# Projecting K and Q of the first token pair one tile at a time, and retuning the planner, in a fused transformer layer

## The chip, the cores and the metric

The kernel runs on one core of one Trainium2 chip. The metric is the device time of one execution in microseconds (us). A run is one execution; a profiled execution also leaves a trace, and its span is some 2 us shorter than its time. Engine names: PE is TensorE, DVE is VectorE, ACT is ScalarE, SP is the queue that issues the DMAs. The profile also records the clock that PE was granted, as a share of the full one; in these runs it is 1.00 or 0.50.

## The reference

One pre-norm transformer layer on 2048 tokens of 1024 columns with 32 heads of 32 columns, and a feed-forward part (FFN) of 3584 columns. Everything is bf16.

```python
def _A_ref(x, wqkv, wo):
    qkv = (x @ wqkv).reshape(B, S, 3, H, Dh)          # H = 32, Dh = 32; cut
    scores = jnp.einsum("bhqd,bhkd->bhqk", q, k) * Dh ** -0.5
    o = jnp.einsum("bhqk,bhkd->bhqd", _softmax(scores), v)
    return o.reshape(B, S, D) @ wo                     # transposes cut
def _B_ref(x, w1, b1, w2, b2):
    return _gelu(x @ w1 + b1) @ w2 + b2
h = x + _A_ref(_layernorm(x), A_wqkv, A_wo)
return h + _B_ref(_layernorm(h), B_w1, B_b1, B_w2, B_b2)
```

## The kernel before

The kernel is a program generator. Python code lists tasks for all engines with estimated durations. A planner then simulates them and fixes the order of instructions on each engine. So a changed estimate can move thousands of instructions, and the diff alone doesn't show which.

Queries are handled in chunks of 256 tokens. A *round* is 8 score matmuls (keys of two token tiles, into PSUM) and two exponentials of 128x1024 on ACT. There are 1024 exponentials. `PT` names the exponentials, and *PV* is their product with V, again on PE. A tile is 128 tokens. The beginning of the program (the *lead*) takes tokens in pairs of tiles: layer norm, transposes (`xnT`), K and Q of the first head group (`KT`, `QT`), V, then a round. `proj_k` and the like take a start column and a width: 256 columns are both tiles.

```python
    jobs = [Job(0, 0, 6, True), Job(0, 1, 5, True)]     # PSUM banks 6 and 5
    for i in range(8):
        ...                                             # cut: layer norm of tiles 2i, 2i+1
        for tt in tts:
            trs.append(tr_tile(tt, "act" if i in ACT_T else "dma"))
        proj_k(group("lead", FULL), 0, 256 * i, 256, "act")      # both tiles at once
        if i < 2:
            q = group("lead", FULL)
            proj_q(q, 0, 256 * i, 256, i, "dve")
        v = group("lead", FULL)
        ...
        proj_v(v, 2 * i, 0, "act")
        jobs[0].round()
```

Later, work of the FFN fills PE between the rounds. Its second matmul (FFN2) reads the weights `w2r` from a ring of 7 slots, one DMA of 512 KB each. One output half `j` needs FC // 4 = 7 such blocks; the two token tiles `t` share them. `PLAN` says in which order the FFN2 groups (`F2[0]` to `F2[3]`, as `(j, t)`) and blocks of the first FFN matmul (the numbers say how many) are offered to PE. `AHEAD` is a look-ahead in us of the planner's own time: a group of matmuls may be begun when its operands will be ready that soon. (The expectations below call it a share.)

```python
    NW1, NW2 = 4, 7
    F2 = [(0, 0), (0, 1), (1, 0), (1, 1)]
    PLAN = [F2[0], 3, F2[1], 4, F2[2], 5, F2[3], 2]
    ...
    def ffn2(R, c, j, t, tail=False):
        if t == 0:
            w2s[c, j] = [w2block(R.w2, B_w2[512 * q:512 * q + 512, 512 * j:512 * j + 512]) for q in range(FC // 4)]
    ...
    AHEAD = 0.15
    ...                                                 # cut, in the planner's choice for PE:
        p.left == 0 and p.ready <= now + AHEAD and all(x.done is not None for x in p.gate)
        and all(x.left == 0 for x in p.dmas)
```

The softmax here doesn't subtract the row's maximum and nothing guards it: scores larger than these inputs give would overflow.

Of the kernel before, what the change touches and what calls it, by code (L numbers as in the profile page):

```python
# [12 lines left out]
P = 128  # L13
# [299 lines left out]
def build_kernel(nc, A_x, A_wqkv, A_wo, B_w1, B_b1, B_w2, B_b2, out):  # L313
# [17 lines left out]
    gr = Graph(N_LANES)  # L331
# [68 lines left out]
    F2 = [(0, 0), (0, 1), (1, 0), (1, 1)]  # L400
# [51 lines left out]
    B_ps = [gr.buf() for _ in range(8)]  # L452
# [5 lines left out]
    hd = nc.dram_tensor("h_scratch", [NC - 1, 2, P, D], BF, kind="Internal").ap()  # L458
    B_hd = [[gr.buf() for _ in range(2)] for _ in range(NC - 1)]

    MM = 0.2150

    def c_dve_ps(n):
        return (120 + n) / 960.0 + 0.02
# [4 lines left out]
    def c_act(n, ap_bias=False):  # L469
        return 0.072 + (0.093 if ap_bias else 0.0) + n / 1200.0  # L470

    EXP = (0.9163, 0.9013)

    def pe(fns, occ, reads=(), writes=(), kind="bg", mode="full", prio=0, after=()):
        return gr.add(E.PE, fns, occ, 0.16, reads, writes, prio, kind, mode, after)
# [3 lines left out]
    def group(name, full=False):  # L479
        g = Group((1, len(groups)), gr.buf())  # L480
        g.full = full
        g.after = ()
        g.name = name
        groups.append(g)
        return g
# [6 lines left out]
    def mm(g, lhsT, rhs, start, stop, reads, cols=(0, 512)):  # L492
        c0, c1 = cols
        occ = MM * (c1 - c0) / 512.0 + 0.0015
        fns = []
        k = rhs.shape[1] if len(rhs.shape) == 3 else 1

        def dst(a, b):
            o = psum[a:b, g.bank, c0:c1]
            return o if k == 1 else o.rearrange("p (k n) -> p k n", k=k)  # L500
        for j in range(4):
            fns.append(lambda p, j=j: p.matmul(dst(32 * j, 32 * j + 32), lhsT[:, 32 * j:32 * j + 32], rhs,  # L502
                                               start=start, stop=stop, tile_position=(0, 32 * j), skip_group_check=True))
        t = grp_pe(g, fns, occ, reads, "col")
        t.alt = [lambda p: p.matmul(dst(0, P), lhsT, rhs, start=start, stop=stop, skip_group_check=True)]  # L505
        if g.full:
            t.fns, t.mode = t.alt, "full"
# [82 lines left out]
    def evacuate(eng, dst, src, n, reads, writes):  # L590
        if eng == "act":
            act(lambda a: a.activation(dst, src(), ACT.Copy), n, reads=reads, writes=writes, prio=-1)  # L592
        else:
            dve(lambda v: v.tensor_copy(dst, src()), c_dve_ps(n), reads=reads, writes=writes, prio=-2)  # L594
# [11 lines left out]
    def x_tile(tt, prio):  # L606
        ap, b = x_slot(tt)
        return dma(ap, x2[tt * P:(tt + 1) * P, :], P * D * 2, writes=b, prio=prio)

    def ln_tiles(tts, prio, on_act=(), after=()):  # L610
        return layer_norm([x_slot(tt) + (xb[:, tt % NXB, :], B_xb[tt % NXB]) for tt in tts], prio, on_act, after)

    def tr_tile(tt, evac):
        if evac != "dma":
            transposes(group("lead", True), xb[:, tt % NXB, :], B_xb[tt % NXB], xnT[:, tt, :, :], B_xnT[tt], evac)
            return
        return dma_t(xnT[:, tt, :, :], xb[:, tt % NXB, :], [B_xb[tt % NXB]], [B_xnT[tt]], prio=-6)

    def proj(grp, which, g, t0, n, col, start=True):
        blk, c = divmod(g * P, 512)  # L620
        blk += WQ if which == 0 else WK
        a, b = t0 // P, (t0 + n) // P
        for dc in range(DC):
            mm(grp, Wall[:, blk, dc, c:c + P], xnT[:, a:b, dc, :], start and dc == 0, dc == DC - 1,
               [B_W[blk][c // P]] + B_xnT[a:b], cols=(col, col + n))

    def proj_k(grp, g, t0, n, evac):
        proj(grp, 1, g, t0, n, 0)
        evacuate(evac, KT[:, g, t0:t0 + n], lambda: psum[:, grp.bank, 0:n], n, [grp.buf], B_KT[g][t0 // 256:(t0 + n) // 256])

    def proj_q(grp, g, t0, n, slot, evac):
        proj(grp, 0, g, t0, n, 0)
        k = n // 256
        evacuate(evac, QT[:, slot:slot + k, :], lambda: psum[:, grp.bank, 0:n].rearrange("p (s t) -> p s t", s=k), n,
                 [grp.buf], B_QT[slot:slot + k])

    def proj_v(grp, tt, q, evac):
        blk, c = divmod(256 * q, 512)
        blk += WV
        for k in range(2):  # L640
            for dc in range(DC):
                mm(grp, xnT[:, tt + k, dc, :], Wall[:, blk, dc, c:c + 256], dc == 0, dc == DC - 1,
                   B_W[blk][c // P:c // P + 2] + [B_xnT[tt + k]], cols=(256 * k, 256 * k + 256))
        dst = V[:, 2 * q:2 * q + 2, tt:tt + 2, :].rearrange("p g t c -> p t g c")
        evacuate(evac, dst, lambda: psum[:, grp.bank, :].rearrange("p (t g c) -> p t g c", t=2, g=2), 512,
                 [grp.buf], [B_V[2 * q][tt // 2], B_V[2 * q + 1][tt // 2]])
# [30 lines left out]
    class Job:  # L677
# [10 lines left out]
        def round(self):  # L688
# [18 lines left out]
            for q in range(2):  # L707
                u = us[q]
                t = act(lambda a, u=u, q=q: a.activation(PT[:, s, 2 * q:2 * q + 2, :], psum[:, 2 * u:2 * u + 2, :], ACT.Exp, bias=0.0, scale=SCALE),  # L709
                    1024, reads=[B_ps[2 * u], B_ps[2 * u + 1]], writes=[B_PT[s][q]], kind="exp")  # L710
                t.occ = EXP[q]
            direct = self.direct or (self.final and r == 7)
# [76 lines left out]
    def wo(R, c):  # L789
        for j in range(2):  # L790
            ws = wo_w(R, j)
            for t in range(2):
                wo_group(R, c, j, t, ws)
# [14 lines left out]
    def ln2(R, c, evac):  # L808
        for t in range(2):
            ln2_tile(R, c, t, evac)  # L810
# [72 lines left out]
    def mixed(R, c1, c2, plan):  # L883
        blk = 0
        for p in plan:
            if isinstance(p, int):
                ffn1(R, c1, range(blk, blk + p))
                blk += p
            else:
                ffn2(R, c2, *p)  # L890
# [22 lines left out]
    for i in range(8):  # L913
        tts = [2 * i, 2 * i + 1]
        if i == 0:
            ln_tiles(tts[:1], LEAD_PRIO)
            first = ln_tiles(tts[1:], LEAD_PRIO, (0,))
        else:
            ln_tiles(tts, 0, (), first)
        for tt in tts:  # L920
            trs.append(tr_tile(tt, "act" if i in ACT_T else "dma"))
            if tt + NXR < NT:
                last_x = [x_tile(tt + NXR, -4)]
        proj_k(group("lead", FULL), 0, 256 * i, 256, "act")
        if i < 2:
            q = group("lead", FULL)
            proj_q(q, 0, 256 * i, 256, i, "dve")
        v = group("lead", FULL)
        if i == 0:
            v.after = q.buf.w  # L930
        proj_v(v, 2 * i, 0, "act")
        jobs[0].round()
        if i == 1:
            jobs[1].round()
        if i >= 1:
            jobs[1].round()
# [30 lines left out]
    def projections(g):  # L967
        proj_q(group(f"pq{g}"), g, 0, 512, slot_of(g, 0), "dve")
        for tc in range(4):
            proj_k(group(f"pk{g}"), g, 512 * tc, 512, "dve")  # L970
        if g > 1:
            for tt in range(0, NT, 4):
                proj_v1(group(f"pv{g}.{tt}", True), tt, g, "dve")
# [20 lines left out]
    def attention(c):  # L994
        for g in range(G):
            attend(g, c)
            c2, g2 = divmod(G * c + g + NQ, G)
            if c2 < NC:
                load_q(g2, c2)

    PLAN = [F2[0], 3, F2[1], 4, F2[2], 5, F2[3], 2]
    wo(R1, 1)
    ffn1(R1, 0, range(FC // 2))
    for c in range(2, NC):
        if c > 2:
            wo(R1, c - 1)
        ln2(R1, c - 1, "dma")
        mixed(R1, c - 1, c - 2, PLAN)
        attention(c)
# [11 lines left out]
    k = R1.w1.k % NW1  # L1021
# [30 lines left out]
    g_next = [0]  # L1052
    qks = [t for t in gr.tasks if t.kind == "qk"]
    PV_START = 6
    AHEAD = 0.15
    HOLD = 3

    def full_array(t):
# [2 lines left out]
    def pick_pe(rd, now, state, up):  # L1061
# [20 lines left out]
        for t in rd:  # L1082
# [10 lines left out]
            else:  # L1093
                p = t.grp
                if p.bank is None and (not new_ok or not ((p is first and n >= len(pvs)) or (
                        p.left == 0 and p.ready <= now + AHEAD and all(x.done is not None for x in p.gate)
                        and all(x.left == 0 for x in p.dmas)))):
# [25 lines left out]
        return warm  # L1123

    num = {t: i for i, t in enumerate(gr.tasks)}
    gr.schedule(pick_pe, switch=0.11382196630878494)

    sems = {e: nc.alloc_semaphore(f"f_{e.name}") for e in (E.PE, E.Activation, E.DVE, E.Pool)}
    lanes = [nc.alloc_semaphore(f"f_lane{i}") for i in range(N_LANES)]
# [28 lines left out]
def bass_sequential_preLN__softmax_full_mha__dense_activation_gelu__prompt_kernel(  # L1158
    nc: bass.Bass,
    A_x: bass.AP,  # L1160
    A_wqkv: bass.AP,
    A_wo: bass.AP,
    B_x: bass.AP,
    B_w1: bass.AP,
    B_b1: bass.AP,
    B_w2: bass.AP,
    B_b2: bass.AP,
    out: bass.AP,
):
    build_kernel(nc, A_x, A_wqkv, A_wo, B_w1, B_b1, B_w2, B_b2, out)  # L1170
# [28 lines left out]
```

## Time and profile before

The median was 1099.68 us in 3 runs (1098.5 to 1100.67). The profile was read in three stages, marked by the exponentials in ACT's timeline:

| stage, kernel before | from where to where | us |
|---|---|---|
| lead | start to the start of the 33rd exponential, from which on ACT is fed | 63.26 |
| middle | to the end of the 1024th exponential (1022.50) | 959.24 |
| tail | to the end of the span (1096.5) | 74.03 |

Three lines of the page matter besides those that the prediction shows: the shares of the chain that ended last by engine, the group of FFN2's matmuls (after the last bar: idle time of PE before them, and what ended most of it), and the loads of FFN2's weights (KB each, median us from issue to landing).

### The profile page before, as it was taken

The numbers are of one execution on the slowest core, as the hardware profiler recorded it, in microseconds if no ns is written. First come the engines' busy times: TensorE is split into PE (matmuls) and PEld (weight loads), VectorE is DVE, ScalarE is ACT, GpSimd is POOL, SyncE is SP. The second block draws the span as 40 slices with busy tenths as digits, with TensorE's granted clock in tenths as the row PEclk, the third lists the DMA queues.
The fourth block names the chain that finished last, engine by engine and source line by source line (L and its number), as shares of the span: only waits on it lengthen the run. The fifth ranks groups of instructions, "written<-read, shape, count | busy, mean of one in ns | idle before, by whom it ended". The sixth has DMA issues, their size and how long they took to land.

```text
span 1096.5 us, 41949 instructions
## 1 busy us (share of the span) xinstructions
PE 1062.1 (97%) x19130; PEld 589.0 (54%) x19135; DVE 822.9 (75%) x1449; ACT 1021.6 (93%) x1135; POOL 17.8 (2%) x33
## 2 busy tenths in 40 slices
PE   7999999999999989999999999999999999999999
PEld 6545555554444655554555455455545544554485
DVE  7456666767767998788788788877887888887562
ACT  5889999999999999999999999999999999999351
POOL 1000000000000000000000000000000000000000
PEclk9999999999999999999999999999999999999999
DMA  7960100013444755577838856765778477968860
GB/s 197 195 159 3 51 3 3 3 41 92 120 122 127 210 133 162 183 242 150 271 113 254 218 169 185 210 208 153 234 162 255 136 224 205 311 186 261 248 224 20
DMA packets 269211, 176.52 MB, mean 161 GB/s; under 512 B 51434, under 2 KB 265066, under 8 KB 269034
## 3 DMA queue, kind: packets, MB, share of 16 engines
q1 hardware_dynamic: 269034, 173.84, 55.4%
q8 instruction: 150, 2.46, 0.9%
q14 instruction: 27, 0.22, 0.1%
HBM read 155.98 MB, written 11.01 MB: 152 GB/s over the span
## 4 chain that ended last, share of the span: by engine, by line
ACT 83%; PE 15%; DMA 1%; DVE 1%; issue 0%; POOL 0%; POOLq 0%; DVEq 0%
ACT PT L709 79%; PE ps L505 8%; ACT a_sq L850 4%; PE ps L502 3%; PE ps L701 1%; PE ps L721 1%; DMA hnT<-xb 1%; PE ps L907 1%; PE ps L740 1%; DVE PS L716 0%; ACT xnT L584 0%; PE ps L581 0%; DVE gT L851 0%; ACT V L592 0%; DVE a_os L878 0%
## 5 line engine op out<-in xcount | busy, mean ns | idle before, releaser
L709 ACT ACTIVATE PT<-ps 128x1024 bf16<-128x1024 f32 x1024 | 953.8, 1164 | 12.7 <-PE ps L701 12.4
L716 DVE TENSOR_TENSOR PS<-PT 128x1024 bf16<-128x1024 bf16 x495 | 327.6, 686 | 83.1 <-ACT PT L709 49.5
L701 PE MATMUL ps<-QT,KT 32*128 32x256 bf16 x4096 | 203.9, 273 | 13.5 <-ACT PT L709 11.5
L505 PE MATMUL ps<-hnT,w1r 128*128 128x256 bf16 x1632 | 209.5, 274 | 2.1 <-DVE gT L832 0.6
L502 PE MATMUL ps<-w2r,gT 128*32 128x512 bf16 x2880 | 192.8, 383 | 1.9 <-issue 0.8
L721 PE MATMUL ps<-PT,V 128*32 128x256 bf16 x4096 | 180.9, 275 | 5.9 <-ACT PT L709 5.0
L505 PEld LDWEIGHTS ps<-hnT,w1r 128*128 128x128 bf16 x1632 | 146.2, 98 | 57.0 <-issue 36.2
L701 PEld LDWEIGHTS ps<-QT,KT 32*128 32x128 bf16 x4096 | 61.3, 92 | 163.5 <-ACT PT L709 141.7
L740 PE MATMUL ps<-PS,ones 128*32 128x256 bf16 x1980 | 139.4, 276 | 2.3 <-DVE PS L716 1.5
L502 PE MATMUL ps<-xnT,Wall 128*32 128x512 bf16 x1888 | 126.0, 381 | 1.3 <-DVE stg L594 1.2
L721 PEld LDWEIGHTS ps<-PT,V 128*32 128x32 bf16 x4096 | 94.4, 96 | 54.5 <-ACT PT L709 24.0
L502 PEld LDWEIGHTS ps<-w2r,gT 128*32 128x32 bf16 x2880 | 67.4, 96 | 71.2 <-issue 26.7
L832 DVE TENSOR_TENSOR gT<-ps,b1f 128x512 bf16<-128x512 f32 x98 | 67.4, 687 | 25.7 <-PE ps L505 24.5
L740 PEld LDWEIGHTS ps<-PS,ones 128*32 128x32 bf16 x1980 | 51.7, 96 | 40.6 <-DVE PS L716 23.4
L505 PE MATMUL ps<-Wall,xnT 128*128 128x128 bf16 (+1 forms) x896 | 69.3, 227 | 0.7 <-ACT xnT L584 0.7
L851 DVE SCALAR_TENSOR_TENSOR gT<-a_sq,gT 128x1024 bf16<-128x1024 bf16 x49 | 59.9, 1222 | 12.3 <-ACT a_sq L850 11.8
L502 PEld LDWEIGHTS ps<-xnT,Wall 128*32 128x32 bf16 x1888 | 43.5, 96 | 46.5 <-issue 15.0
L505 PEld LDWEIGHTS ps<-Wall,xnT 128*128 128x128 bf16 x896 | 55.2, 98 | 16.3 <-issue 10.7
L502 PE MATMUL ps<-w1r,OT 128*32 128x512 bf16 x896 | 62.2, 381 | 0.5 <-DVE OS L752 0.2
L848 DVE SCALAR_TENSOR_TENSOR a_sq<-a_sq,gT 128x1024 bf16<-128x1024 bf16 x49 | 59.8, 1221 | 0.7
L850 ACT ACTIVATE a_sq<-a_sq 128x1024 bf16<-128x1024 bf16 x49 | 58.9, 1203 | 0.0
L749 DVE STREAM_TRANSPOSE DT<-ps 128x256 f32<-128x256 f32 x64 | 28.5, 445 | 20.1 <-PE ps L740 20.1
(76 smaller groups left out, 570.7 us busy)
## 6 DMA issues: line engine op xcount, KB each, us to landing
w2r<-in_B_w_dram SPq DMA_DIRECT2D x105, 512.0 KB, 6.0
w1r<-in_B_w_dram SPq DMA_DIRECT2D x102, 512.0 KB, 4.6
w1r<-in_A_wo_dram SPq DMA_DIRECT2D x28, 512.0 KB, 4.4
wk<-in_B_w_dram SPq DMA_DIRECT2D x9, 512.0 KB, 5.9
xrb<-in_A_x_dram SPq DMA_DIRECT2D x16, 256.0 KB, 4.9
Wall<-in_A_wqkv_dram SPq DMA_DIRECT2D x16, 256.0 KB, 5.1
wv<-in_B_w_dram SPq DMA_DIRECT2D x8, 512.0 KB, 6.9
a_x<-in_A_x_dram SPq DMA_DIRECT2D x28, 128.0 KB, 3.4
```

The costliest lines, as they stand in the source:

```text
L502: fns.append(lambda p, j=j: p.matmul(dst(32 * j, 32 * j + 32), lhsT[:, 32 * j:32 * j + 32], rhs, start=start, stop=stop, tile_position=(0, ...
L505: t.alt = [lambda p: p.matmul(dst(0, P), lhsT, rhs, start=start, stop=stop, skip_group_check=True)]
L701: fns.append(lambda p, i=i, hh=hh, r0=r0: p.matmul(psum[:, 2 * us[hh // 2] + hh % 2, 256 * i:256 * i + 256], KT[r0:r0 + 32, g, 256 * r + P ...
L709: t = act(lambda a, u=u, q=q: a.activation(PT[:, s, 2 * q:2 * q + 2, :], psum[:, 2 * u:2 * u + 2, :], ACT.Exp, bias=0.0, scale=SCALE), 102 ...
L716: dve(lambda v: v.tensor_tensor(PS[:, z, :, :], PT[:, s, :, 0:256], PT[:, s, :, 256:512], ALU.add), c_dve(1024, 2), reads=B_PT[s], writes= ...
L721: fns.append(lambda p, i=i, hh=hh: p.matmul(psum[32 * hh:32 * hh + 32, self.bank, 0:256], V[:, g, 2 * r + i, 32 * hh:32 * hh + 32], PT[:, ...
L740: fns.append(lambda p, i=i, hh=hh, src=src: p.matmul(psum[32 * hh:32 * hh + 32, self.bank, 256:512], ones32[:, :], src[:, hh, :], start=False,
L749: dve(lambda v: v.transpose(DT[f][:], psum[:, self.bank, 256:512]), c_dve_ps(256), reads=[self.buf], writes=[B_DT[f]], prio=-1)
L832: gate[c] = dve(lambda v, xh=xh, fc=fc, grp=grp: v.tensor_tensor(xh, psum[:, grp.bank, :].rearrange("p (f n) -> p f n", f=2), b1f[:, fc:fc ...
L848: dve(lambda v: v.scalar_tensor_tensor(v4(sq), v4(sq), C2, xh, ALU.add, ALU.mult), c_dve(n), reads=[b_sq] + b_xh, writes=[b_sq], prio=GP)
L850: gate[c] = act(lambda a: a.activation(sq, sq, ACT.Tanh, bias=0.0, scale=K2 / 2), n, writes=[b_sq], prio=-1, kind="tanh")
L851: t = dve(lambda v: v.scalar_tensor_tensor(xh, v4(sq), 1.0, xh, ALU.add, ALU.mult), c_dve(n), reads=[b_sq] + b_xh, writes=b_xh, prio=GP)
```

## The change

The intent: before the first scores, K and Q of both first tiles are projected after the second tile's transposes, in 16 matmuls of 256 columns. If tile 0's halves are projected as soon as tile 0 is there, tile 1 adds only half. Q's first half needs a PSUM bank, and bank 5 of the second job is idle then. The rest of the diff retunes the planner. (Hunk heads and some context are cut.)

```diff
-    MM = 0.2150
+    MM = 0.2158
-    EXP = (0.9163, 0.9013)
+    EXP = (0.9189, 0.9039)
+    def proj_tiles(grp, which, g, t0, n):
+        for k in range(0, n, P):
+            proj(grp, which, g, t0 + k, P, k)
     def proj_k(grp, g, t0, n, evac):
-        proj(grp, 1, g, t0, n, 0)
+        (proj_tiles if n == 256 and t0 == 0 else lambda *a: proj(*a, 0))(grp, 1, g, t0, n)
     def proj_q(grp, g, t0, n, slot, evac):
-        proj(grp, 0, g, t0, n, 0)
+        (proj_tiles if n == 256 and t0 == 0 else lambda *a: proj(*a, 0))(grp, 0, g, t0, n)
             q = group("lead", FULL)
+            if i == 0:
+                q.bank, q.buf = 5, B_ps[5]
-    PLAN = [F2[0], 3, F2[1], 4, F2[2], 5, F2[3], 2]
+    PLAN = [2, F2[0], 4, F2[1], 4, F2[2], 4, F2[3]]
-    AHEAD = 0.15
+    AHEAD = 0.3
-    gr.schedule(pick_pe, switch=0.11382196630878494)
+    gr.schedule(pick_pe, switch=0.11267389115514913)
```

## The prediction

> **What bounds the kernel now.** I read the windows table first, then the chain of waits of the first 80 us, then the timeline of the first tiles, and last the waits of ACT.
>
> The windows table (each engine's busy time in stretches of 40 us, its instructions in brackets, then the granted clock, DMA share and GB/s):
>
> ```profile
> 0.00:40.00 40.00, 32.56 (x451) 24.01 (x451) 31.30 (x92) 26.84 (x35) 6.78 (x17) 1.00 0.84 195
> 40.00:80.00 40.00, 39.22 (x727) 20.69 (x727) 14.64 (x28) 34.85 (x42) 0.00 (x0) 1.00 0.86 183
> 80.00:120.00 40.00, 39.85 (x822) 23.20 (x814) 25.28 (x47) 40.00 (x45) 0.00 (x0) 1.00 0.09 28
> ...
> 800.00:840.00 40.00, 38.87 (x748) 18.47 (x736) 30.22 (x62) 39.12 (x44) 1.10 (x2) 1.00 0.79 205
> ...
> 1000.00:1040.00 40.00, 38.17 (x540) 18.08 (x531) 23.71 (x46) 23.14 (x25) 1.54 (x2) 0.96 0.76 230
> 1040.00:1080.00 40.00, 39.89 (x295) 28.89 (x296) 23.24 (x24) 18.41 (x35) 0.00 (x0) 1.00 0.52 171
> ```
>
> The fourth busy figure is ACT. It is full from 80 us until 1000 us and not before or after, so there are three stages. A **lead** lasts until ACT is fed without a gap (63.26 us in the timeline, start of a run of 19 exponentials that takes 17.52 us, a pitch of 0.922). A **middle** of some 959 us, until the last exponential ends at 1022.5, is ACT's own work. A **tail** of 74 us follows, in which PE is dense. The change helps only if it brings the 63.26 forward, takes a stall out of ACT's middle, or shortens PE's tail.
>
> The chain of waits (start, duration, engine, what) shows how the lead starts:
>
> ```profile
> 8.07 1.45 PE ps L907 x26
> 9.52 0.46 PE ps L581 x8
> 9.98 0.02 issue
> 10.00 1.03 ACT xnT L584
> 11.04 0.14 issue
> 11.17 2.56 PE ps L505 x22
> 13.73 0.36 PE ps L701 x8
> 14.09 0.02 issue
> 14.11 1.94 ACT PT L709 x2
> 16.05 0.50 ACT V L592
> 16.55 0.04 issue
> 16.59 0.40 PE ps L721 x8
> 17.00 0.17 PE ps L581
> 17.17 0.02 issue
> 17.20 1.95 ACT xnT L584 x2
> ```
>
> Tile 1 is transposed, copied out by ACT, and only then are K and Q of both tiles projected (16 matmuls of 256 columns, followed by 6 of V). The first scores come at 13.66 and the first exponentials at 14.11. After that the lead is a chain of 16 rounds. A round's scores wait for both exponentials of the round before, and the exponentials wait for the scores, so a round costs at least 2.45 us (scores 23.36, 25.80). From 13.66 the sixteenth could begin at 13.66 + 15 x 2.45 = 50.4; the timeline has it at 58.09. 7.7 us are lost on the way, 4.7 of them between the first and the second round.
>
> ACT's middle is nearly closed: its waits add up to 0.3 + 1.3 + 1.4 = 3.0 us between 63 and 1022 us. The longest is this one (windows of 2 us):
>
> ```profile
> 1002.00:1004.00 2.00, 1.08 (x32) 0.35 (x22) 1.99 (x3) 2.00 (x3) 0.00 (x0) 1.00 1.15 326
> 1004.00:1006.00 2.00, 1.59 (x28) 0.57 (x24) 0.84 (x2) 2.00 (x3) 0.00 (x0) 0.71 1.07 293
> 1006.00:1008.00 2.00, 2.00 (x24) 0.78 (x20) 1.27 (x2) 2.00 (x3) 0.00 (x0) 0.50 0.72 227
> ```
>
> PE had little to do (1.08 of 2 us), its clock was then granted at half, and the score matmuls that ACT waited for came 1.4 us late.
>
> **What the Trainium skill says.** TensorE: Matmul & The Clock Gate, section "Wait — 56ns, not 53.3ns?", gives a warm matmul 55.6 ns at 128 columns and 215.7 at 512. The trace agrees: 26 warm-up matmuls of 128 columns took 1.45 us (56 ns each), and 256 columns cost (1.85 - 1.42)/4 = 107 ns, from chain pieces of 16 and 12 matmuls. So halves cost no more than wholes per column. The same page, Part 3, "The mechanism", says that matmuls start and end in program order; hence a projection put ahead of a transpose holds it up. Its section "What's actually happening" says that an idle PE falls to half clock; the 0.50 above agrees. ScalarE: Activation LUTs, "What ACT_TABLE_LOAD costs", has 186 ns + 0.833 per column less 93 of overlap: 946 ns at 1024 columns; the trace has 922.
>
> **The change, part by part.** Columns of projection stay equal: 16 matmuls of 256 become 32 of 128. By the order of instructions 8 of them (Q, tile 0, in bank 5) now stand before tile 1's transposes, 8 (K, tile 0) behind them, and 16 wait for tile 1.
>
> *Second tile.* 16 x (107 - 56) = 0.82 us come off the path. But Q of tile 0 needs xnT of tile 0, which ACT finished at 9.12; with the 0.15 us from ACT to PE seen at 11.02 to 11.17 it starts at 9.27, takes 8 x 0.056 = 0.45, and with one warm-up matmul the transposes start at 9.78, not 9.36. That is 0.42 back. The net is 0.40: QT is ready to copy at 12.72 in place of 13.12. Seven V matmuls (was six) stand before the scores; they end at 12.49 + 0.1 + 7 x 0.107 = 13.35. First scores near 13.35 to 13.4, a gain of 0.3.
>
> *Second round.* Before, 7 of the 8 transposes of tile 2 stood ahead of the PV matmuls that wait for V. Now PV comes first and all 16 transposes follow. PV moves up 0.3 to 16.28, takes 0.33, a transpose group 0.45: ACT gets tile 2 at about 17.25, against 17.20. The 0.3 is gone.
>
> *Rounds 3 to 16.* The planner has reshuffled them. Before the fifth scores K's last two matmuls now come after the PV that waits for the fourth exponentials: 0.33 + 0.22 + 0.21 + 0.2 of latency + 0.39 of K's copy, about 0.9 us later than before. A copy of V (0.60) now falls between the two exponentials of round 7, some 0.6 more. Against this, in rounds 11, 13 and 15 K is projected a round earlier, so its 0.39 us copy falls into ACT's gap: 3 x 0.4 = 1.2 back. Sum over the lead: 0.05 + 0.9 + 0.6 - 1.2 = +0.3; the change-over to the second head group gains 0.1. So **lead +0.2**, give or take 0.7.
>
> *Middle.* Exponentials and tanh are equal in number. The new constants and plan spread FFN work differently: PE changes mode 1190 times instead of 1215, and just before the last rounds there is FFN2 work left, where before rounds 503 and 504 had only 0.9 to 1.0 us of work each. The dip at 1004 us and its 1.4 us should go. Four gaps between scores of about 3.8 us of work now exist, against one before, which may each cost ACT some tenths. **Middle -1.2**, from 3.0 of stalls to about 1.8.
>
> *Tail.* The order leaves 67 full-array FFN2 matmuls of the chunk before last for the tail where 64 were: 3 x 0.216 = **+0.65**, as nothing there waits for anything but PE.
>
> Sum: 0.2 - 1.2 + 0.65 = -0.35, hence about 1099.3 us.
>
> **The rivals.** (1) The gain survives: if DVE's layer norms, which in 15 to 20 us are 4.92 of 5 us busy, set the rounds, then all that follows moves with the earlier QT copy (DVE stood idle 0.78 us before it), and the 0.4 us reach 63 us whole; with the dip gone, 1097.5. For it: the next layer norm's first step stands behind that copy on DVE. Against: the chain runs through ACT and PE, not DVE. (2) The reshuffled lead loses more than I reckon, because the plan expects transposed tiles at other times than they come; each misplaced wait costs half a round, 1.2 us: 1101 to 1102. (3) Clock dips move rather than vanish. One at 405 us cost ACT nothing, one at 1004 cost 1.4; a new one where ACT has no reserve would make it 1101. For it: after the change the order still has rounds of 0.9 to 1.2 us of PE work around round 200.
>
> **Range and chances.** The parts are worth at most 2 us each, and the runs before spread from 1098.5 to 1100.67. Errors of 0.7 (lead), 1.2 (middle) and 0.5 (tail), with the runs' own 1, make about 1.8 us; 8 in 10 gives 1096.5 to 1102. Two per cent would be 22 us, more than the whole possible loss in the lead, so "same" is nearly sure.
>
> **What would show it right or wrong.** Right: tile 1's transposes start near 9.8, first scores near 13.4, second round's exponentials within 0.2 of 21.27; the last lead scores at 58 to 59; ACT full from about 63.5; ACT's waits between there and the last exponential under 2 us with no dip near 1004; from the last exponential to the end about 0.6 us more than 74.0. Wrong: ACT full before 62 or after 65, a dip that stalls ACT in a new place, or waits for weights in the tail.

## More of the kernel before

```profile
ACT 83%; PE 15%; DMA 1%; DVE 1%; issue 0%; POOL 0%; POOLq 0%; DVEq 0%
...
L502 PE MATMUL ps<-w2r,gT 128*32 128x512 bf16 x2880 | 192.8, 383 | 1.9 <-issue 0.8
...
w2r<-in_B_w_dram SPq DMA_DIRECT2D x105, 512.0 KB, 6.0
```

ACT carries the chain. FFN2's matmuls wait for no weights worth naming. A block of weights is under way for 6.0 us in the median.

## The result, and the profile after

The changed kernel is correct and took 1102.47 us (median of 4 runs, 1100.91 to 1102.86). The kernel before, beside it, took 1099.74 (4 runs, 1098.5 to 1100.67). The ratio is 1.0023, 95% interval 1.0006 to 1.0040. A ratio here is the mean time of one kernel's fast runs over that of the other's of the same rounds, so it isn't quite the ratio of the medians quoted beside it. By the 2% rule the two are the same; by the interval the changed kernel is slower by some tenths of a per cent.

| us, from the profiled executions | before | after | difference | predicted |
|---|---|---|---|---|
| lead (start of the 33rd exponential) | 63.26 | 64.56 | +1.30 | +0.2 |
| middle | 959.24 | 961.93 | +2.69 | -1.2 |
| tail | 74.03 | 74.59 | +0.56 | +0.65 |
| span | 1096.5 | 1101.1 | +4.55 | -0.35 |

The two profiled executions took 1098.32 and 1102.86 us, one at the low and one at the high end of the spreads. Their difference is therefore larger than that of the medians, 2.7 us, and the stages below share out the larger one. One profile of a kernel against another of the same kernel differs too: the middle of the changed kernel is 961.93, 959.98 and 961.64 us in the three that were taken.

**Lead.** The chain of waits of the changed kernel (start, duration, engine, what):

```profile
9.22 0.61 PE ps L505 x8
9.82 0.06 PE ps L911
9.88 0.45 PE ps L581 x8
...
11.00 2.28 PE ps L505 x31
13.27 0.36 PE ps L705 x8
...
17.13 1.95 ACT xnT L584 x2
19.07 0.05 issue
19.12 2.94 PE ps L505 x14
22.06 0.36 PE ps L705 x8
```

Q of tile 0 (9.22) now stands ahead of tile 1's transposes (9.88), and the first scores come at 13.27 instead of 13.73. That is the intended gain. But the 14 projection matmuls at 19.12 take 2.94 us, 210 ns each, twice the 107 ns of the prediction. The reason is in the windows table (busy time of PE, PEld, DVE, ACT and POOL, then the granted clock, DMA share, GB/s), changed kernel:

```profile
14.90:18.30 3.40, 1.49 (x25) 1.11 (x26) 3.40 (x12) 2.36 (x4) 0.29 (x1) 1.00 0.43 154
18.30:21.70 3.40, 3.07 (x15) 1.81 (x15) 2.14 (x6) 1.15 (x2) 0.41 (x1) 0.50 0.15 31
```

and the same stretches of the kernel before:

```profile
14.90:18.30 3.40, 1.96 (x29) 1.12 (x27) 3.40 (x12) 2.75 (x5) 0.25 (x1) 1.00 0.42 143
18.30:21.70 3.40, 2.88 (x29) 2.00 (x30) 2.74 (x7) 1.64 (x3) 0.45 (x1) 1.00 0.14 34
```

After, PE was busy for 1.49 of 3.40 us (0.44), and the whole next window was granted half the clock. Before, it was busy for 1.96 (0.58), and the clock stayed whole. I call such a window a *dip*.

**Middle.** Here are the page's three lines of the changed kernel that answer to those of before:

```profile
ACT 67%; PE 29%; DVE 2%; DMA 1%; issue 1%; SPq 0%; POOL 0%; POOLq 0%; DVEq 0%
...
L502 PE MATMUL ps<-w2r,gT 128*32 128x512 bf16 x2868 | 193.1, 381 | 3.3 <-DMA w2r<-in_B_w_dram 2.5
...
w2r<-in_B_w_dram SPq DMA_DIRECT2D x105, 512.0 KB, 6.7
```

PE's share of the chain doubled from 15% to 29%, at ACT's cost, and most of what FFN2's matmuls wait for is now the DMA of their weights. The windows table shows where ACT lost time; the prediction's table has 1000 to 1040 us for before.

```profile
400.00:440.00 40.00, 36.33 (x612) 19.31 (x612) 36.72 (x54) 39.29 (x44) 0.00 (x0) 0.91 0.46 112
920.00:960.00 40.00, 37.83 (x748) 18.82 (x748) 26.99 (x52) 38.39 (x43) 1.10 (x2) 1.00 0.94 254
1000.00:1040.00 40.00, 37.76 (x615) 18.03 (x608) 28.81 (x52) 27.54 (x31) 1.10 (x2) 1.00 0.79 240
```

ACT (the fourth busy figure) should read 40.00 in the first two rows, as it does before. It lost 0.7 us in the first, where a dip of two windows (407.4 to 414.2) stands in place of one (404.1 to 407.5), and 1.6 us in the second, at a whole clock. In the third row the clock is 1.00 where before had 0.96: the dip at 1004 is gone, as predicted. All of ACT's waits in the middle add up to 4.6 us, against 2.9 before. That is 1.7 of the 2.7 us; the other 1.0 us lies in ACT's busy time (957.2 against 956.2 us), and its cause is open. The chain of the changed kernel in the second stretch:

```profile
935.87 0.33 PE ps L705 x8
936.20 0.57 PE ps L502 x8
936.77 0.49 SPq L523
...
938.07 8.21 DMA w2r<-in_B_w_dram
...
946.33 0.62 PE ps L502 x8
...
947.65 9.27 ACT PT L713 x10
```

and of the kernel before, in the same stretch:

```profile
924.59 12.85 ACT PT L709 x14
937.43 0.94 ACT a_sq L850
938.37 13.76 ACT PT L709 x15
```

Before, the chain is ACT alone. After, a slot of the ring came free when PE had read it at 936.77, its new block took 8.21 us to land, and PE's matmuls of the next half waited for it, with the scores behind them. PE's timeline shows why the block was asked for so late. Before, 64 matmuls of the first FFN matmul (944.8 to 957.7) stand between the halves `j` = 0 and `j` = 1. After, 216 FFN2 matmuls follow each other without any of them (922.2 to 947.9): the last 40 of `F2[0]`, all 112 of `F2[1]` and the first 64 of `F2[2]`, which is the other half. With a ring of exactly one half, nothing could be loaded in advance.

### The profile page after: what moved, and what is told of

The parts are those of the page before. It is cut to its first block, busy times and chain, and to the rows that moved or that the text cites. A ratio compares the mean times of both kernels' runs of the same rounds, so it can differ in the third digit from the quotient of the medians.

```text
span 1101.1 us, 41954 instructions
## 1 busy us (share of the span) xinstructions
PE 1061.1 (96%) x19142; PEld 592.5 (54%) x19142; DVE 822.3 (75%) x1449; ACT 1022.6 (93%) x1135; POOL 17.9 (2%) x33
## 4 chain that ended last, share of the span: by engine, by line
ACT 67%; PE 29%; DVE 2%; DMA 1%; issue 1%; SPq 0%; POOL 0%; POOLq 0%; DVEq 0%
ACT PT L713 64%; PE ps L505 11%; PE ps L502 10%; PE ps L705 4%; PE ps L725 2%; ACT a_sq L854 2%; PE ps L744 1%; DMA w2r<-in_B_w_dram 1%; DVE PS L720 1%; PE ps L911 1%; DVE a_sq L852 0%; DVE gT L836 0%; ACT xnT L584 0%; PE ps L581 0%; DVE DT L753 0%
## 5 line engine op out<-in xcount | busy, mean ns | idle before, releaser
L713 ACT ACTIVATE PT<-ps 128x1024 bf16<-128x1024 f32 x1024 | 953.9, 1148 | 13.6 <-PE ps L705 13.4
L502 PE MATMUL ps<-w1r,OT 128*32 128x512 bf16 x896 | 59.4, 381 | 1.4 <-DVE hch L790 0.8
```

Source lines behind the costliest of these rows:

```text
L502: fns.append(lambda p, j=j: p.matmul(dst(32 * j, 32 * j + 32), lhsT[:, 32 * j:32 * j + 32], rhs, start=start, stop=stop, tile_position=(0, ...
L713: t = act(lambda a, u=u, q=q: a.activation(PT[:, s, 2 * q:2 * q + 2, :], psum[:, 2 * u:2 * u + 2, :], ACT.Exp, bias=0.0, scale=SCALE), 102 ...
```

## The experiments

All ran with 5 rounds, beside the kernel before. Stage figures are of each profiled execution. "Lead" is the start of the 33rd exponential; "first" is that of the first, because the clock's first release wanders between 4.3 and 7.5 us from profile to profile and moves everything after it.

| run | median us | ratio to before, 95% | first | lead | middle | tail |
|---|---|---|---|---|---|---|
| e1_fill | 1106.31 | 1.0079 [1.0058, 1.0099] | 14.39 | 64.84 | 962.34 | 74.66 |
| e2_swap | 1101.89 | 1.0042 [1.0024, 1.0059] | 14.68 | 64.87 | 962.34 | 74.71 |
| e3_lead_only | 1106.62 | 1.0083 [1.0066, 1.0100] | 14.67 | 66.20 | 959.19 | 79.24 |
| e4_retune_only | 1106.98 | 1.0085 [1.0065, 1.0104] | 14.19 | 63.42 | 961.83 | 78.23 |
| e5_after_again | 1101.18 | 1.0028 [1.0013, 1.0043] | 14.60 | 64.99 | 959.98 | 74.67 |
| e6_hoist | 1095.63 | 0.9980 [0.9962, 0.9999] | 14.50 | 63.65 | 957.46 | 73.91 |
| e7_before_midfill | 1098.07 | 0.9994 [0.9976, 1.0011] | 14.94 | 65.56 | 957.24 | 73.90 |
| e8_after_midfill | 1104.31 | 1.0056 [1.0039, 1.0073] | 14.60 | 65.07 | 962.82 | 74.72 |
| e9_after_oldplan | 1099.08 | 1.0009 [0.9992, 1.0026] | 14.67 | 65.06 | 958.34 | 73.78 |
| e10_after_oldahead | 1105.53 | 1.0068 [1.0049, 1.0088] | 14.58 | 66.06 | 962.01 | 74.94 |
| e11_before_newplan | 1105.44 | 1.0068 [1.0050, 1.0085] | 13.92 | 63.07 | 962.27 | 78.11 |
| e12_hoist_fill | 1095.24 | 0.9974 [0.9958, 0.9990] | 13.03 | 63.73 | 957.43 | 73.90 |
| e13_after_now2 | 1099.75 | 1.0029 [1.0009, 1.0048] | 13.51 | 64.34 | 959.51 | 74.59 |
| e14_oldplan_now2 | 1097.33 | 1.0001 [0.9985, 1.0016] | 14.30 | 64.69 | 957.99 | 72.91 |
| e15_oldahead_now2 | 1105.80 | 1.0077 [1.0062, 1.0093] | 14.66 | 66.18 | 963.66 | 74.94 |
| e16_after_third | 1102.91 | 1.0054 [1.0034, 1.0074] | 13.70 | 64.64 | 961.64 | 74.66 |

e1 to e4 shared their runs of before, e5 to e12 likewise (but for one run more), and e13 to e16 were on a third chip. Within such a set, times may be compared directly.

### The lead: is it the dip?

**e1_fill** puts 24 idle matmuls (the identity times itself, read by nobody) into PE's order ahead of the first PV matmuls, so that the window before 18.3 us isn't nearly empty.

```diff
+    at = seq.index(pvs[0])
+    fill = Task(E.PE, [lambda p: p.matmul(psum[:, 5, 0:P], ident[:], ident[:], start=True, stop=True) for _ in range(24)],
+                0.0, 0.0, 0, "warm", "full")
+    ...                                             # cut: what the fill waits for; orders counted anew
+    seq.insert(at, fill)
```

> The changed kernel with 24 idle-data matmuls of 128 columns (24 x 0.056 = 1.3 us) put into PE's gap of 1.44 us ahead of the first PV; every other instruction keeps its place. Theory A (in the changed lead the gap before the first PV let the PE clock fall to half at 18.3 us, and the 14 projection matmuls after it took 2.94 us in place of 1.70): the profile shows no half clock before 40 us, the second scores come at about 20.8 in place of 21.99, ACT is fed without a gap from about 63.3 in place of 64.6, and the kernel is 1.2 us faster than the changed one (about 1101.2). Rival B (the order itself costs it: PV and then sixteen transposes, the split K projection): nothing moves, 1102.5.

It took 1106.31 us. Its profile has no dip at 18.3 but one at 26.8, and the lead is 64.84. In this profile the clock's windows began late, at 6.3 us, so a dip at 18.3 could not come in any case, and whether the fill prevents one there stays untested. But the lead lost as much with a dip at 26.8 as with one at 18.3, so it isn't this one window that decides it. Why its timed runs were 4 us slower than the changed kernel's I did not find out; the profiled one was among its fastest.

**e2_swap** moves tile 2's first transposes back ahead of the first PV matmuls, as in the kernel before.

```diff
+    tr2 = [t for t in seq if t.grp is groups[tr_group] and t.order is not None][:DC]
+    for t in tr2:
+        seq.remove(t)
+    at = seq.index(pvs[0])
+    seq[at:at] = tr2
+    ...                                               # cut; above too: how tr_group is found
```

> The changed kernel with tile 2's eight transposes put back ahead of the first PV, as the kernel before has seven of them; nothing else moves. Theory A: PE's longest gap there is cut from 1.44 to about 0.9 and the dip may go, and ACT can copy tile 2 at about 16.1 in place of 17.13, so the second scores come 1.2 (dip) to 2 us earlier, near 20.0 to 20.8, and ACT is fed by 62.5 to 63.4: about 1100.5 to 1101.3. Rival B (the rounds 3 to 16 absorb it, since their K, V and layer norms were planned for later): the second scores come earlier but the sixteenth do not, 1102.3.

1101.89 us, lead 64.87 with a dip at 27.2: within the spread of the changed kernel (64.56 to 64.99 in three profiles). The place of these transposes isn't what costs.

Over all profiles, every one of the 12 with the changed lead has a dip in it, at 18 or at 27 us by the phase of the windows; of the 4 with the lead of before one has (e7_before_midfill). What a dip costs shows where the same lead came with and without one. From first to 33rd exponential the lead of before takes 49.14 us without (before) and 50.61 with a dip (e7); the lead of e6 and e12 takes 49.15 without and 50.70 with. So a dip costs about 1.5 us. The changed lead takes 50.90 (after), always with a dip.

The phase of the windows matters, though. Where the first full clock came before 5 us, all 3 changed leads have a dip and none of the 3 leads of before. Where it came after 5.9 us, all 9 changed leads have one, but so has the only lead of before (e7), and there ACT is fed at 65.56 us against 64.99 and 65.06 in e5 and e9. So the +1.30 of the table holds for the early phase. Which phase the timed runs had isn't recorded.

### Lead edits or retuned planner?

**e3_lead_only** has the two edits of the lead and the constants and plan of before; **e4_retune_only** has the new constants and plan and the lead of before.

```diff
 e3: the changed kernel with
-    MM = 0.2158 ; EXP = (0.9189, 0.9039) ; AHEAD = 0.3 ; switch=0.11267389115514913
+    MM = 0.2150 ; EXP = (0.9163, 0.9013) ; AHEAD = 0.15 ; switch=0.11382196630878494
-    PLAN = [2, F2[0], 4, F2[1], 4, F2[2], 4, F2[3]]
+    PLAN = [F2[0], 3, F2[1], 4, F2[2], 5, F2[3], 2]
 e4: the kernel before with the same lines the other way round
```

> The kernel before with only the two edits of the first pair (one tile at a time, Q in bank 5); the planner's constants and the plan of the FFN as before. If the first pair is what costs time: slower than before by about 1.3 us or more (the same order of PV and transposes, the same dip), near 1101. If the constants and the plan cost it (ACT's stalls in its middle): same as before or faster, 1099 to 1099.7.

> The kernel before with only the constants (MM, EXP, switch, AHEAD) and the plan of the FFN changed; K and Q of the first pair projected as before. If the retuning costs what the trace shows in ACT's middle and tail (2.7 + 0.6 us): about 1103. If the first pair costs it: near 1099.7, with the second scores at 20.8.

Each half alone costs 9 us (1106.62 and 1106.98), while both together cost 2.5 to 6. Their tails are 79.2 and 78.2 us. In the traces PE needs, from the last scores to its own end, 78.9 and 77.7 us, against 73.7 before and 74.2 after. So the new constants go with the new lead: they bring the tail back to 74. The middle tells something else. With the plan of before it is 959.19 (e3), with the new one 961.83 (e4). And in e4 no wait of PE between 64 and 1020 us names `w2r` at all, a point to keep for theory P below.

**e5_after_again** and **e16_after_third** are the changed kernel once more, beside other runs.

> The changed kernel itself, to have its distribution beside the others on one chip. The four runs so far have a granted clock of 0.995 (three half-clock windows of 3.41 us each) and 1100.9 to 1102.9. Every run of before with 0.998 (one window) took 1095.1 to 1095.9, with 0.997 (two) 1096.5 to 1098.0, with 0.994 (four) 1097.2 to 1101.2. If the windows were all of the difference, runs of the changed kernel at 0.997 or 0.998 would take 1095 to 1098; if the order costs time of its own, they stay over 1099.

> The changed kernel again, beside e13: 1101 to 1102.5, waits for w2r of 5 to 7 us, middle 960 to 962 us, a half-clock window in the lead.

1101.18 us (ratio 1.0028) and 1102.91 (1.0054). The loss is real: three intervals leave out 1, and the ratios lie between 1.002 and 1.006. Dips aren't all of it. Two runs of e5 had a granted clock of 0.998 and 0.997 and took 1100.13 and 1101.16 us, where the kernel before took 1095.2 to 1097.4 at these clocks beside them. PE's waits for `w2r` between 64 and 1020 us are there each time: 6.5 us of matmuls and weight loads together in the first profile, 6.1 in e5 and 7.0 in e16, against 0.5 in the kernel before. (Weight loads overlap matmuls, so these sums measure how often PE waits and aren't lost time.) The table of waits of e16_after_third (us in total, times, longest) has them so:

```profile
PEld ps L502 <- DMA w2r<-in_B_w_dram: 4.3, 4, 1.7
...
PE ps L502 <- DMA w2r<-in_B_w_dram: 2.7, 3, 1.2
```

### The idea alone, with the planner's order of before

**e6_hoist** takes the kernel before with its order as planned, splits the first pair's 16 K and Q matmuls in halves after planning, and puts tile 0's halves directly *behind* tile 1's transposes, K in bank 4 and Q in bank 5.

```diff
+    q0.bank, k0.bank = 5, 4
+    for grp, blk in ((k0, WK), (q0, WQ)):
+        for dc, t in enumerate([t for t in seq if t.grp is grp]):
+            e = Task(E.PE, [half(0)], t.occ, t.lat, 0, "bg", "full")     # tile 0
+            e.deps = t.deps - late                                       # late: tile 1's xnT
+            early.append(e)
+            t.fns = [half(1)]                                            # tile 1
+    at = max(i for i, t in enumerate(seq) if t.grp is tr1) + 1
+    seq[at:at] = early
+    ...                                               # cut; above too: definitions, further dependencies
```

> The order of before on all engines, with only the intent of the change: K and Q of tile 0 (16 matmuls of 128 columns, 0.9 us) done behind tile 1's transposes while ACT copies tile 1, Q in bank 5, K in bank 4; the 16 for tile 1 stand where the 16 of 256 columns stood. Theory A (the idea is worth its 0.8 us, what costs time is the reordering that the planner made around it): first scores 0.7 to 0.8 us earlier than the 13.66 of before, second scores some 0.5 to 0.8 earlier, ACT's middle and the tail as before, 0.3 to 0.8 us faster than before. Rival B (an earlier first exponential leaves PE idle longer, and it loses its clock in the lead, as in every kernel with the edit so far): a half-clock window before 40 us and 1 us slower than before. Rival C (DVE's layer norms set the later rounds): second scores earlier, sixteenth not: same as before.

1095.63 us, ratio 0.9980 [0.9962, 0.9999]: faster than the kernel before. The middle (957.46) and the tail (73.91) are those of before without its dip at 1004. The lead's gain has to be read at the same release of the clock. e12_hoist_fill below (released at 4.35 us) has its first exponentials at 13.03, e11 with the lead of before (4.33) at 13.92, and e13 with the changed lead (4.30) at 13.51. So the idea is worth 0.9 us there, and the changed lead gets 0.4 of it. From the first to the 33rd exponential e6 takes 49.15 us as before takes 49.14: with the order of before, the gain reaches the 33rd whole. It explains 0.9 of the some 2 us; the rest is open.

### The middle: idle matmuls at the dips

**e7_before_midfill** is the kernel before with 13 idle matmuls in each of the rounds 197 to 200, 502 and 503; **e8_after_midfill** is the changed kernel with the same in the rounds 198 to 202.

```diff
+    for k in [k for a, b in [(197, 201), (502, 504)] for k in range(a, b)]:
+        for i, n in ((pos[order[k]] + 1, 8), (pos[order[k + 1]], 5)):
+            ...   # cut: take the free one of PSUM banks 6 and 7
+            put.append((i, f, k, b))              # f: n matmuls of the identity
```

> The kernel before with 13 idle-data matmuls of 128 columns (0.7 us) in each of six rounds in which PE has under 1.25 us of work (197 to 200 and 502, 503), in the PSUM bank that is free there. Theory: the half-clock windows at 404 and 1005 us come from those rounds, so the profile shows none there, the stall of ACT at 1007 (2.6 us between two exponentials) goes, and the kernel is 1 to 2 us faster than before, with clocks of 0.998 and more. Rival (the windows come from something else, or the matmuls get in the way of the scores): no change or slower.

> The changed kernel with the same filling in rounds 198 to 202. Theory: the double half-clock window at 407 us goes, the loss of some 1.2 us of ACT between 411 and 414 us with it, clocks of 0.998; 1 to 1.5 us faster than the changed kernel. What stays above before (1.5 to 3 us) is then owed to the lead and to stalls that no clock explains. Rival: no change.

e7 took 1098.07 us (0.9994, no difference to be seen). The dip at 1005 was gone and ACT gained about 1.6 us there, but it lost about 2.0 around a dip at 409. e8 took 1104.31, slower than the changed kernel: the dip at 407 shrank to one window, but ACT had only 37.83 busy us in these 40. At 408.98 a fill had waited 1.51 us for its PSUM bank, with the scores behind it. So neither fill shows that dips in the middle make the changed kernel slower.

### The middle: the plan, `AHEAD`, or the waits for weights?

**e9_after_oldplan** is the changed kernel with the plan of before, **e10_after_oldahead** the changed kernel with the `AHEAD` of before, and **e11_before_newplan** the kernel before with the new plan.

```diff
 e9:  the changed kernel with
-    PLAN = [2, F2[0], 4, F2[1], 4, F2[2], 4, F2[3]]
+    PLAN = [F2[0], 3, F2[1], 4, F2[2], 5, F2[3], 2]
 e10: the changed kernel with
-    AHEAD = 0.3
+    AHEAD = 0.15
 e11: the kernel before with
-    PLAN = [F2[0], 3, F2[1], 4, F2[2], 5, F2[3], 2]
+    PLAN = [2, F2[0], 4, F2[1], 4, F2[2], 4, F2[3]]
```

> The changed kernel with the FFN order (the plan) of the kernel before; everything else as changed, and PE's order is the same as the changed kernel's until about 87% of the program. Theory P (the new plan puts the last token tile's second FFN matmul group at a chunk's end, so that the next chunk's first such group asks for its weights before they have landed): PE's waits for the DMA of w2r in the middle fall from about 6 us (changed kernel) to about 0.5 us (kernel before), the middle from exp 33 to the last exp falls from 961.9 to about 958 to 959.5 us, and the time is 2 to 3 us under the changed kernel, about 1098 to 1099 beside a kernel before of 1097.5. Rival H (the share by which FFN work runs ahead, 0.3 in place of 0.15, asks for them early): waits and time as in the changed kernel, 1101 to 1102.5.

> The changed kernel with the share by which FFN work runs ahead put back from 0.3 to 0.15, everything else as changed. Theory P: waits for the DMA of w2r stay at 5 to 7 us and the time stays at 1101 to 1102.5. Rival H: they fall to about 0.5 us and the time to 1098 to 1099.

> The kernel before with the changed kernel's plan alone; PE's order is the same as before until about 88% of the program. By count of the order, 78.0 us of PE work are left after the last scores, where before has 73.8, so both theories expect a tail near 78 and at least 4 us more in all. Theory P: PE also waits about 6 us for the DMA of w2r, the middle is 961.5 to 962.5 us, and the time is about 1103 to 1107. Rival H: those waits stay near 0.5 us, the middle 955 to 958 (work moved from it into the tail), the time about 1098 to 1102.

e9 came in at 1099.08 us, with a mean 2.1 us under e5's on the same chip (1099.18 and 1101.27; by the spread of the runs between 1.0 and 3.2). PE waits for no `w2r` at all in its middle, and the middle is 958.34. So the plan costs the changed kernel 2 us; theory P's time and its waits were right. The `AHEAD` of 0.3 is no culprit but a help: without it (e10) the kernel is slower by another 4.4 us in the mean (1105.72 against 1101.27).

One part of theory P failed. e10 has only 3.7 us of waits for `w2r` and e11 only 1.3, and their middles are as long as the changed kernel's (962.01 and 962.27). So the plan lengthens the middle even where weights are hardly waited for, and in e4, by name, not at all. The names may miss some: amid FFN2's matmuls PE pauses 0.63 us at 932.2 in e11 and 0.38 us at 930.0 in e4, for nothing that the profile shows. The texts for e9 and e11 also err in one point: by the traces PE's order parts from that of the other kernel at 433 and 430 us, not at 87% of the program, so the plan acts on the whole second half.

**e13_after_now2**, **e14_oldplan_now2** and **e15_oldahead_now2** take away the wait alone. The order on every engine and all DMAs stay, but FFN2's matmuls (all chunks but the last) stream the identity, four times over, in place of `w2r`, and so don't wait for its DMA. Their outputs are wrong, which doesn't matter for the times.

```diff
+    same = ident[:].unsqueeze(1).to_broadcast([P, 4, P])
+    for u, (grp, lhsT, fc, load) in no_w2.items():        # FFN2's matmuls, after planning
+        ...                                               # cut: same shape, `same` in place of w
+        u.deps.discard(load)
```

> Wrong result on purpose: the changed kernel, same order on every engine and all its DMAs, but the second FFN matmuls of all chunks but the last stream the identity (broadcast four times) in place of w2r, so none of them waits for the weights' DMA. Theory W (the waits for the weights cost the time): PE's waits for w2r are 0, the middle falls from 960 to 962 us to 957.5 to 959, and the time is 1.5 to 3 us under the changed kernel run beside it. Rival O (the order as such costs it): the middle stays at 960 to 962 us and the time within 0.7 us of the changed kernel.

> Wrong result on purpose; control: e9 (the changed kernel with the plan of before) with the same replacement. It has 0.8 us of waits that name w2r, so both theories expect it within 0.7 us of e9 (1099.1, middle 958.3). If it is over 1 us faster, the replacement itself speeds PE and e13 must be read against this.

> Wrong result on purpose: e10 (the changed kernel with the share 0.15) with the same replacement. e10 has 3.7 us of waits for w2r. Theory W: the middle falls from 962.0 by 1 to 2.5 us and the time from 1105.5 to about 1103 to 1104.5. Rival O: unchanged, 1105 to 1106.

e13 against e16 on the same chip: mean 1100.42 against 1103.22 us, 2.8 less (by the spread of the runs between 0 and 5.6), and the middle 959.51 against 961.64, 2.1 less. The control e14 stands at 1.0001, e9 at 1.0009, so the replacement itself is worth some 0.9 us, uncertain by 2.5; its middle moved by 0.35 (957.99 after 958.34). These differences are no larger than that between two profiles of one kernel, so here is the place itself, 930 to 950 us, in the changed kernel, in e9 and in e13 (columns as above):

```profile
930.00:950.00 20.00, 17.83 (x351) 8.20 (x344) 11.56 (x24) 18.39 (x21) 0.00 (x0) 1.00 1.01 288
930.00:950.00 20.00, 20.00 (x339) 11.19 (x336) 15.51 (x28) 20.00 (x23) 0.00 (x0) 1.00 0.92 287
930.00:950.00 20.00, 19.59 (x376) 9.36 (x369) 13.14 (x25) 20.00 (x23) 0.00 (x0) 1.00 1.01 266
```

ACT loses 1.6 us in the changed kernel and nothing in the other two. In the six profiles with plan, constants and lead edits as changed (with e1, e2, e5, e8 and e16) the loss there is 1.3 to 2.0 us; in the seven with the plan of before it is 0 to 0.9. (e10 loses 0.2 and e11 1.2.) The waits for the weights therefore cost the changed kernel about 1.5 to 2 us (theory W). In e15 nothing was gained (1105.80 after 1105.53, middle 963.66 after 962.01): with `AHEAD` at 0.15 the new plan's middle is long for another reason, and there rival O stands. e13's middle also stays 1.2 us over e9's, within what profiles of one kernel differ by. What in the new plan's order costs the rest stays open.

### A version that beats both

**e12_hoist_fill** is e6 with 13 idle matmuls in each of the rounds 502 and 503, to keep the dip near 1005 away.

```diff
 e6 with e7's block of idle matmuls, and
-    for k in [k for a, b in [(197, 201), (502, 504)] for k in range(a, b)]:
+    for k in [k for a, b in [(502, 504)] for k in range(a, b)]:
```

> The kernel before with only tile 0's K and Q ahead (the run e6_hoist, 1095.6), and 13 idle matmuls in each of the rounds 502 and 503. If the half-clock window near 1005 us would have come, it is gone and about 1 to 1.5 us with it: 1094 to 1096; if it would not have come, as in e6's profile, the fill costs nothing or up to 0.5 us: 1095.5 to 1096.5. It also repeats e6's lead: at or under the kernel before by 1 to 2.5 us if e6's gain was real, level with it if it was chance of the windows.

1095.24 us, ratio 0.9974 [0.9958, 0.9990]. It's correct and faster than both kernels. It can't be told from e6, and neither profile has a dip near 1005, so the fill can't be credited with anything. Its lead had a dip at 18.0 and still reached ACT's full feed at 63.73.

## Why the prediction was wrong

The class, within 2%, was right. The time was not: 1102.47 us lies just above the range's end of 1102.0, and the sign of the difference was wrong.

**Second tile: right.** Transposes were expected at 9.78 and came at 9.88; the first scores were expected at 13.35 to 13.4 and came at 13.27. The reckoning that Q's early half takes back 0.42 of the 0.82 us is borne out by e12, which puts the halves behind the transposes: at the same release of the clock its first exponentials are 0.9 us earlier than before, those of the changed lead 0.4.

**Second round: right but for the dip.** The exponentials were expected within 0.2 of 21.27 and came at 22.44. In e5, where no dip fell into this stretch, first and second scores are 7.55 us apart against 7.16 before, +0.39, and the text had 0.3.

**Rounds 3 to 16: right.** The terms +0.9, +0.6 and -1.2 measured +0.98 (fourth to fifth scores, 3.97 against 2.99), +0.48 (seventh to eighth, 2.93 against 2.45) and -1.29 (eighth to sixteenth, 20.27 against 21.57, rounded). The summands that the text gives for the +0.9 add up to 1.35; how 0.9 comes of them it doesn't say.

**Lead +0.2: mis-sized, by a term left out.** It measured +1.30. The sum has no term for a half clock in the lead, and one came: it cost 1.2 us in the 14 projection matmuls alone (2.94 in place of 1.70), and 1.5 by the pairs of leads above. Leads that both have a dip, after and e7, differ from first to 33rd exponential by only 50.90 - 50.61 = 0.3. With first exponentials 0.45 earlier, that would be -0.15 in place of +0.2. The step reckoned what PE waits for, but didn't ask what clock PE gets when it waits more. Rival (3) named the mechanism and looked for it in rounds near 200. That an early gain can reach the 33rd exponential whole, as rival (1) had it, only e6 shows.

**Middle -1.2: the step that failed.** It measured +2.69. The step is the sum of ACT's stalls, "from 3.0 of stalls to about 1.8": they came to 4.6. The half that was argued from the dip at 1004 came true, in part by luck: the dip is gone, but e6, whose middle has the order of before, has none there either. The failing sentence is "Four gaps between scores of about 3.8 us of work now exist, against one before, which may each cost ACT some tenths". (With the dip's 1.4 gone, 1.8 leaves 0.2 us for all four.) It counts PE's work between scores, as if every matmul there could start when its turn comes. Their weights hadn't landed. The waits for `w2r` (e13 against e16), brought by the new plan (e9 against e5), cost ACT 1.6 us between 930 and 950 us in this profile, and the timed runs differ by 2.1 (e9) and 2.8 us (e13); the prediction took that plan for a way of spreading work. The text did name waits for weights as a sign of error, but in the tail. A second, smaller miss: the dip near 405, put at no cost, became two windows long, and ACT lost 0.7 us in that stretch of 40 us. The 1.0 us in ACT's busy time had no term either. With the plan of before, the changed kernel's middle is 958.34 (e9), but that of e6 and e7, with nothing retuned, is 957.46 and 957.24: so no run shows the gain of 1.2.

**Tail +0.65: right.** +0.56, and no wait for weights in it.

**Sum.** -0.35 became +4.55 in the profiles: 1.1 of the error is the lead, 3.9 the middle, -0.1 the tail. In the medians it became +2.7. The range was too narrow above all because errors of the middle were thought to be tenths per gap.

The reason in the planner, that it put FFN2 groups back to back because its model lands a block sooner than the chip does, is only argued. Its model takes 2.0 us and 512 KB at 260 GB/s, about 4 us for a block that meets no other; the profile has a median of 6.7.

## What to carry to other kernels

When a change reorders matmuls, ask for each one that moves forward whether its operands can have landed: find the DMA's time from issue to landing, and what has to be read before its buffer is free. A ring that holds exactly one group's operands can load nothing ahead for a different group that follows at once: here it cost ACT 1.3 to 2.0 us in one place. And try the idea alone, with everything else frozen, before retuning around it: here the bare idea ran 0.2% faster than before (e6, e12), and the retuned version 0.2 to 0.5% slower.

## What the Trainium skill lacked or had wrong

- "TensorE: Matmul & The Clock Gate", section "What's actually happening", gives half clock as the state "after ≥1 idle window (~3.4µs)". The length agrees (3.41 us in the clock records), but a window need not be idle: in these leads, windows in which PE was busy for 0.44 (after), 0.52 (e7), 0.53 (e5) and 0.54 (e12) of the time were followed by half clock, and windows at 0.56 (e7), 0.57 (e12) and 0.58 (before, e5, e6) were not. The share alone doesn't decide it, though: one at 0.53 in e14 (16.2 us) was not followed by half clock, one at 0.57 in e2 (23.8 us) was. The shares are sums of the matmul records over each window.
- The same section says that the free-running window makes the first transition vary by ±500 ns. In these profiles the first full clock came between 4.3 us (e11, e13) and 7.5 us (e6), while the first matmul stood at 1.5 us, and this moved first exponentials by about a microsecond (13.51 in e13, 14.68 in e2) and decided where dips could fall.
